# A linear recurrence with a routed expert layer on one core: early router rows searched per 256 columns, the last router step apart, weights and more zero fills inside a new hand-ordered list

## Chip, cores and metric

The kernel runs on one core of one Trainium2 chip. The metric is the device time of one execution in microseconds (us); less is better. The core has five engines with a queue each: TensorE (PE, with its weight loads shown as PEld), VectorE (DVE), ScalarE (ACT), GpSimd (POOL) and SyncE (SP), which here issues nearly all DMAs. Engines run their own queues in order and wait for each other by semaphores.

## What is computed

The input is a batch of 4 sequences of 5056 tokens with 256 channels, float32. First a gated linear recurrence runs over each sequence, and then its 20224 result rows go through a top-1 routed layer of 8 experts, in which each expert keeps only its 80 most certain tokens. All other output rows are zero.

```
sig_r, sig_i = sigmoid(r_gate), sigmoid(i_gate)
a_t = exp(8 * sig_r * log(sigmoid(a_param)))
x_gated = sqrt(max(1 - a_t*a_t, 1e-6)) * sig_i * x
h_t = a_t * h_(t-1) + x_gated_t             # along the sequence, per channel
logits = h @ w_gate                         # [20224, 8]
expert = argmax(logits);  gate = softmax(logits)[expert]
for each expert e: keep the 80 tokens of e with the largest gate
    out[token] = gate * (relu(h[token] @ w1[e]) @ w2[e])     # 256 -> 1024 -> 256
out[all other tokens] = 0
```

## The kernel before

**Data.** `Y` is one large SBUF tensor of 50 slots of 128 x 1024 float32. Slots 0 to 39 end up holding the recurrence's result, channel-major, in 40 units `u` of 512 tokens (the last has 256). Until then the slots hold loaded inputs and intermediate values; the tables `SLOTS` say which slot serves `r`, `i`, `x` and the decay `a` of each unit. Slots 40 to 49 are extra and later hold expert weights (`wbuf`, slots 40 to 47) and scratch (`scr`, slots 48 and 49).

**The main phase** is a list, `ORDER`, of tokens, each a task; every engine executes its part in the order of the list (`tc.manual_schedule`). SP's DMAs follow the same list. The tasks of unit u: `Lr`, `Li`, `Lx` load 512 KB each; `Tr` transposes r on PE into PSUM; `tr` is the tanh on ACT; `e` the decay (two Exp on ACT); `q` its square (POOL); `s` the root (ACT); `ti` a tanh of i (ACT); `u` or `v` the gated input, on POOL (L152, L153) or on DVE (L155); `Tu` transposes it on PE; `xg` multiplies by the norm (DVE L163); `y` is the scan (DVE L171), which carries its state from unit to unit. A number after the dot of `e`, `q`, `s`, `ti`, `u`, `v` says how many units one instruction covers. ACT pays a table load each time it changes between Exp/Tanh and Sqrt.

**The router.** `G` g forms logits of four units (2048 tokens) with eight matmuls in fp32 (two instructions each, L233). `R` s.k is stage k of router step s; a step covers two groups, so five steps cover ten groups (the last group has units 36 to 39):

```
stages = (r_copy, r_turn, r_max, r_exp, r_first, r_sum, r_recip, r_gate_, r_back, r_store)
```

They copy the logits to `lg` (ACT L237), transpose them (PE L241), find and subtract the maximum (DVE L252, L253), exponentiate (ACT L258), mark the first largest expert (DVE L262 to L264), add up and invert (POOL L269 to L272, DVE L275), multiply the mark with the gate (POOL L278), transpose back (PE L283) and store into `rows` (ACT L287). `rows` has 128 partitions (8 experts x 16, by token mod 16) and 1264 columns: 1024 "early" columns from groups 0 to 7, 240 late ones from groups 8 and 9, and between them 16 places (`K1`) for the largest early values. One PSUM tile (`ps_g`, one buffer) serves all steps, and one `lg`.

**The end of the list.** `T` (`early_top`) finds the 16 largest of the 1024 early columns of each partition: largest eight, their indices, replace, largest eight, indices (L292 to L294). `Z` writes 256 KB of zeros to the output (L218); 79 of them cover the output, 45 stand in the list, and the other 34 are issued after it, behind the first eight weight loads (L320, L323).

**After the list.** `top16` over the 16 early winners and 240 late columns gives 16 candidates per partition. Exact ranks among the 16 partitions of an expert follow (DVE L403, L410, ACT L404), a one-hot selection (DVE L420, PE L426), and a branch (L476) that jumps over a slow general path unless a partition could hold more chosen tokens than were searched. Then each of ACT, POOL and DVE reads its share of an expert's 80 column numbers into registers (L499, one register load of 28 or 24 values) and copies those columns one by one (L505, L506); PE multiplies (L520, L522) and POOL scatters the rows to the output (L533). Weights of experts 2 to 7 are loaded as buffers come free.

Of the kernel before, what the change touches and what calls it, by code (L numbers as in the profile page):

```python
# [15 lines left out]
P = 128  # L16
C = 512
# [7 lines left out]
STEPS = ((0, 1), (2, 3), (4, 5), (6, 7), (8, 9))  # L25
SLOTS = dict(r=(1, 2, 3, 4, 5, 10, 14, 16, 21, 22, 13, 24, 29, 31, 33, 27, 37, 38, 41, 21, 22, 35, 44, 45, 46, 30, 40, 48, 31, 33, 49, 43, 36, 46, 47, 44, 49, 43, 42, 47),
             i=(6, 8, 9, 19, 20, 9, 19, 27, 30, 20, 32, 34, 18, 19, 23, 20, 40, 34, 43, 32, 36, 24, 27, 33, 42, 32, 36, 47, 34, 44, 32, 41, 40, 48, 42, 45, 37, 46, 45, 48),
             x=(11, 13, 15, 8, 11, 23, 25, 15, 26, 28, 35, 36, 30, 25, 26, 18, 42, 28, 47, 29, 48, 25, 26, 43, 28, 38, 41, 29, 42, 45, 38, 34, 35, 41, 38, 40, 48, 41, 40, 44),
             a=(0, 7, 12, 17, 18, 6, 7, 8, 12, 9, 11, 17, 14, 15, 16, 19, 23, 17, 20, 31, 49, 34, 23, 37, 24, 25, 27, 35, 28, 37, 30, 31, 32, 33, 34, 35, 36, 38, 41, 39))
# [29 lines left out]
    xg36.1 y36.0 Z u38.1 R3.3 Tu37.0 Z tr38 R3.4 Tu37.1 Z tr39 Z e38.1 y36.1 Z Z xg37.0 e39.1 R3.5 Tu38.0 Z xg37.1 ti39.1 Z q38.1 y37.0 Z s38.1 R3.6
    Z Tu38.1 y37.1 R3.7 Z q39.1 Z R3.8 xg38.0 Z u39.1 xg38.1 Z s39.1 y38.0 Z Z R3.9 Tu39.0 y38.1 Tu39.1 Z G8 Z xg39.0 xg39.1 Z y39.0 Z y39.1 Z T Z  # L60
    G9 Z Z Z R4.0 Z R4.1 Z Z Z Z R4.2 Z R4.3 Z R4.4 R4.5 R4.6 R4.7 R4.8 R4.9
# [18 lines left out]
def moe_kernel(ctx, tc, x, r_gate, i_gate, a_param, w_gate, w1, w2, out, capacity=80):  # L80
# [14 lines left out]
    tiny = const.tile([P, 58], F32, name="tiny")  # L95
# [84 lines left out]
    mx = h1[:, 144:176]; sm = h1[:, 176:208]; total = h1[:, 208:240]  # L180
# [25 lines left out]
    eidx = tiny[:, 38:54].bitcast(U32); ecol = tiny[:, 22:38]  # L206
# [13 lines left out]
    st = {}  # L220
    LAST = -(-NU // 4) - 1
    exx = lg[:, C // 2:]
    def width(g): return min(512, (N - 2048 * g) // 4)
    def logits(g):

        s = plan.step_of[g]; k = g - plan.steps[s][0]; last = g == plan.steps[s][-1]
        if k == 0: st['pl'] = ps_g.tile([P, 512], F32, name="pl")
        us = range(4 * g, min(4 * g + 4, NU))
        for n in sorted({ntok(u) for u in us}, reverse=True):
            part = [u for u in us if ntok(u) == n]; c0 = (part[0] - 4 * g) * P; last_part = last and n == min(ntok(u) for u in us)  # L230
            for h in range(2):
                for j in range(4):
# [5 lines left out]
    def r_turn(s):  # L238
        st['pt'] = pt = st['pl'].rearrange("p (b k) -> p b k", b=4)
        w = width(plan.steps[s][0])  # L240
        for b in range(4): nc.tensor.transpose(pt[:w // 4, b], lg[:, b:w:4], ident)  # L241
# [351 lines left out]
```

## Time and profile before

| | us |
|---|---|
| median of 3 runs (lowest, highest) | 332.15 (331.56, 332.41) |
| the profiled execution, its own time | 329.29 |
| span of its trace (first to last instruction) | 327.5 |
| mean granted TensorE clock | 0.792 |

| engine | busy us | share of span |
|---|---|---|
| PE | 222.6 | 68% |
| DVE | 222.7 | 68% |
| ACT | 231.2 | 71% |
| POOL | 231.5 | 71% |

The DMAs moved 100.7 MB, 307 GB/s over the span; the queue of SP's DMAs was busy 86% of the time that 16 DMA engines have. The shares are averages over the main phase (to about 225 us), the router's end and the search (to about 251 us), a stretch with almost nothing (251 to 256 us), and the experts (to the end). So each stretch has to be read by itself. The TensorE clock is given as a share of full speed: 1.00 is 2.4 GHz and 0.50 is 1.2 GHz.

### The profile page before, as it was taken

The page shows a single profiled execution, that of the slowest core. Times are in us where ns is not written, and L with a number is a line of the kernel's source. Part 1 is how long each engine was busy: PE and PEld are TensorE (multiplying, and loading weights), DVE is VectorE, ACT ScalarE, POOL GpSimd, SP SyncE. Part 2 cuts the span into 40 slices and gives each one's busy share as a digit, 9 for nine tenths or more (in the row PEclk, how much of TensorE's full clock was granted, in tenths as well). Part 3 has the DMA queues.
Part 4 walks back from the last instruction along what each step waited for, and adds up shares of the span by engine and source line. Part 5 has one row for each costly group of instructions (what it writes and reads, how often), then busy time and mean ns, then how long its engine had stood idle before and what let it go on. Part 6 is the DMA issues. An engine that isn't in the chain of part 4 may idle for free. (4 is left out here: it accounts for less than half of the span.)

```text
span 327.5 us, 5668 instructions
## 1 busy us (share of the span) xinstructions
PE 222.6 (68%) x1400; PEld 169.1 (52%) x1400; DVE 222.7 (68%) x515; ACT 231.2 (71%) x454; POOL 231.5 (71%) x358
## 2 busy tenths in 40 slices
PE   3663838496669855798644776348253668999994
PEld 3562833255565343754523326222142558999994
DVE  1047978968579993998659796799684174466611
ACT  6999999989969999689659998891131063453500
POOL 2494999789699999799996989981253167453712
PEclk9957678578579995599975797957757675999999
DMA  7999999999987479896996879999999942999940
GB/s 251 409 404 345 385 412 410 409 370 393 366 327 234 162 260 372 274 309 220 313 366 215 277 208 355 392 374 296 370 375 375 335 165 67 301 353 336 343 149 20
DMA packets 52532, 100.70 MB, mean 307 GB/s; under 512 B 4368, under 2 KB 32912, under 8 KB 52496
## 3 DMA queue, kind: packets, MB, share of 16 engines
q1 hardware_dynamic: 52112, 99.64, 86.0%
q0 software_dynamic: 384, 0.66, 0.6%
q8 instruction: 13, 0.21, 0.3%
q14 instruction: 23, 0.19, 0.2%
HBM read 78.91 MB, written 21.36 MB: 306 GB/s over the span
## 5 line engine op out<-in xcount | busy, mean ns | idle before, releaser
L171 DVE TENSOR_TENSOR_SCAN Y<-Y,pu 128x512 f32<-128x512 f32 (+4 forms) x86 | 97.5, 1169 | 0.4
L160 PE MATMUL pu<-ident,Y 128*128 128x128 f32 x316 | 61.2, 334 | 44.9 <-DVE Y L171 33.6
L141 POOL TENSOR_TENSOR Y<-Y 128x1024 f32<-128x1024 f32 (+2 forms) x29 | 75.2, 2608 | 16.4 <-ACT Y L138 15.9
L160 PEld LDWEIGHTS pu<-ident,Y 128*128 128x128 f32 x316 | 44.4, 172 | 68.3 <-issue 46.3
L153 POOL TENSOR_TENSOR Y<-Y 128x1024 f32<-128x1024 f32 (+2 forms) x25 | 72.9, 2916 | 2.2 <-POOL Y L152 0.2
L124 PE MATMUL pr<-ident,Y 128*128 128x128 f32 x316 | 55.9, 341 | 26.9 <-DMA Y<-in_r_gate_dram 19.0
L124 PEld LDWEIGHTS pr<-ident,Y 128*128 128x128 f32 x316 | 49.1, 181 | 32.4 <-ACT Y L126 14.1
L163 DVE SCALAR_TENSOR_TENSOR pu<-Y,pu 128x512 f32<-128x512 f32 (+1 forms) x80 | 51.2, 676 | 16.5 <-ACT Y L144 11.7
L138 ACT ACTIVATE Y<-Y,tiny 128x512 f32<-128x512 f32 (+2 forms) x58 | 52.4, 961 | 3.0 <-POOL Y L271 2.4
L520 PE MATMUL ph<-Y 128*128 128x80 f32 x256 | 45.7, 273 | 4.4 <-DMA out_dram<-Y 3.0
L522 PE MATMUL po<-Y,rows 128*80 128x128 f32 x256 | 48.3, 282 | 0.0
L148 ACT ACTIVATE Y<-Y 128x1024 f32<-128x1024 f32 (+2 forms) x29 | 38.7, 1359 | 7.8 <-DMA Y<-in_i_gate_dram 7.6
L126 ACT ACTIVATE Y<-pr 128x1024 f32<-128x1024 f32 (+1 forms) x40 | 39.1, 1005 | 7.1 <-PE pr L124 7.1
L520 PEld LDWEIGHTS ph<-Y 128*128 128x128 f32 x256 | 40.6, 206 | 5.0 <-POOL Y L506 3.4
L505 ACT COPY Y<-Y 128x2 f32 x224 | 22.8, 191 | 26.2 <-issue 23.7
L506 POOL COPY Y<-Y 128x2 f32 x192 | 24.3, 200 | 24.0 <-issue 16.1
L152 POOL TENSOR_SCALAR Y<-Y 128x1024 f32<-128x1024 f32 (+2 forms) x25 | 33.8, 1352 | 9.7 <-ACT Y L148 7.3
L233 PE MATMUL pl<-Y 128*32 128x512 f32 (+2 forms) x176 | 37.3, 986 | 2.0 <-ACT rows L287 2.0
L144 ACT ACTIVATE Y<-Y 128x1024 f32<-128x1024 f32 (+2 forms) x32 | 38.0, 1248 | 0.4 <-POOL Y L141 0.3
L522 PEld LDWEIGHTS po<-Y,rows 128*80 128x80 f32 x256 | 29.8, 158 | 0.0
L506 DVE COPY Y<-Y 128x2 f32 x224 | 24.7, 178 | 7.2 <-issue 7.0
L155 DVE SCALAR_TENSOR_TENSOR Y<-Y 128x1024 f32<-128x1024 f32 x9 | 18.0, 2002 | 17.0 <-ACT Y L148 14.8
(131 smaller groups left out, 159.5 us busy)
## 6 DMA issues: line engine op xcount, KB each, us to landing
out_dram<-Y SPq DMA_DIRECT2D x79, 256.0 KB, 4.7
Y<-in_r_gate_dram SPq DMA_DIRECT2D x39, 512.0 KB, 6.3
Y<-in_i_gate_dram SPq DMA_DIRECT2D x39, 512.0 KB, 6.8
Y<-in_x_dram SPq DMA_DIRECT2D x39, 512.0 KB, 5.8
Y<-in_moe_w_dram SPq DMA_DIRECT2D x32, 512.0 KB, 5.0
Y<-in_r_gate_dram SPq DMA_DIRECT2D x1, 256.0 KB, 7.6
Y<-in_x_dram SPq DMA_DIRECT2D x1, 256.0 KB, 7.4
Y<-in_i_gate_dram SPq DMA_DIRECT2D x1, 256.0 KB, 5.2
```

The costliest lines, as they stand in the source:

```text
L124: nc.tensor.transpose(pr[:, h, b:nb * P:nb], rr[:, b, h * P:(h + 1) * P], ident)
L126: nc.scalar.activation(rslot(u), prs.pop(u)[:, :, :ntok(u)], AF.Tanh, scale=0.5)
L138: nc.scalar.activation(a[:, :, h], z[:, :, h], AF.Exp, scale=L[:, h:h + 1], bias=L[:, h:h + 1])
L141: nc.gpsimd.tensor_tensor(pair('r', u, m), a, a, op=ALU.mult)
L148: nc.scalar.activation(i, i, AF.Tanh, scale=0.5)
L153: nc.gpsimd.tensor_tensor(v, i, v, op=ALU.mult)
L160: nc.tensor.transpose(pu[:, b:nb * P:nb], tmb('x', u)[:, b, h * P:(h + 1) * P], ident)
L163: nc.vector.scalar_tensor_tensor(pu, rslot(u)[:, h], 0.5e-3, pu, op0=ALU.max, op1=ALU.mult)
L171: nc.vector.tensor_tensor_scan(y[:, s0:s1], a[:, s0:s1], q[:, s0:s1], init, op0=ALU.mult, op1=ALU.add)
L506: else: eng.tensor_copy(dst, src)
L520: nc.tensor.matmul(ph[:, c % (FC // 2)], w1v(e1)[:, h, c * P:c * P + P], XG[:, e1, h], start=(h == 0), stop=(h == 1))
L522: nc.tensor.matmul(po[:, h, :P], h2T[:, c], w2v(e2)[:, c, h * P:h * P + P], start=(c == 0), stop=(c == FC - 1))
```

## The change

1. `T` is gone. Behind router steps 0 to 3 a task `P` s finds the eight largest of that step's 256 columns and their indices. Near the end, `M0` (DVE) picks the 16 largest of the 4 x 8 = 32 values and marks which cell they come from, `M1` and `M2` (POOL) turn that into column numbers.
2. Eight per 256 columns may miss a ninth. The row's largest "eighth" is kept, and the flag for the general path is raised where a chosen candidate is not above it: on DVE a maximum, a comparison, a product and a sum stand where one comparison stood.
3. The last router step is split: step 4 has group 8 alone, step 5 group 9 alone, with its own PSUM tile and its own SBUF buffers (slot 49). Group 9's matmuls come in two parts, `Ga` for units 36 to 38 and `Gb` for unit 39 alone; `Ca` copies the first part. In step 5 the sum and the gate's product are on DVE.
4. The list is a new one throughout, with new slots. The 8 weight loads stand in it (`W0` to `W7`), and 63 zero fills, the first behind `xg14.0` (before: behind `y32.0`). Up to the last input load the list has 49 zero fills (before: 12), behind it 14 (before: 33), and 16 come after the list (before: 34). Tasks by kind, of those whose count changes:

| | e pairs, singles | s pairs, singles | ti pairs, singles | u pairs, singles (POOL) | v singles (DVE) |
|---|---|---|---|---|---|
| before | 11, 18 | 8, 24 | 11, 18 | 6, 19 | 9 |
| after | 10, 20 | 6, 28 | 10, 20 | 4, 21 | 11 |

In both lists ACT changes to the root's table 11 times.

```diff
-STEPS = ((0, 1), (2, 3), (4, 5), (6, 7), (8, 9))
+STEPS = ((0, 1), (2, 3), (4, 5), (6, 7), (8,), (9,))
...
-    Z Tu38.1 y37.1 R3.7 Z q39.1 Z R3.8 xg38.0 Z u39.1 xg38.1 Z s39.1 y38.0 Z Z R3.9 Tu39.0 y38.1 Tu39.1 Z G8 Z xg39.0 xg39.1 Z y39.0 Z y39.1 Z T Z
-    G9 Z Z Z R4.0 Z R4.1 Z Z Z Z R4.2 Z R4.3 Z R4.4 R4.5 R4.6 R4.7 R4.8 R4.9
...
+    u38.1 R3.8 y36.0 e38.1 Z Z y36.1 Tr39 R3.9 Z Tu37.1 tr39 xg37.0 G8 Z e39.1 q38.1 xg37.1 W0 s38.1 y37.0 q39.1 W1 y37.1 u39.1 P3 W2 Tu38.0 Tu38.1
+    s39.1 xg38.0 W3 R4.0 Tu39.0 xg38.1 R4.1 y38.0 Z W4 y38.1 Tu39.1 Z R4.2 Ga Z xg39.0 R4.3 xg39.1 y39.0 Z y39.1 W5 R4.4 R4.5 Gb Ca M0 W6 R5.0 R5.1
+    W7 R5.2 M1 Z R4.6 R5.3 R5.4 Z Z R5.5 R4.7 R5.6 M2 R4.8 Z R5.7 R5.8 Z R4.9 R5.9
 """
...
-    mx = h1[:, 144:176]; sm = h1[:, 176:208]; total = h1[:, 208:240]
+    mx = h1[:, 122:154]; sm = h1[:, 154:186]; total = h1[:, 186:218]
+    cell = h1[:, 218:250]; eighth = h1[:, 250:251]; cell0 = h1[:, 251:255]
...
+    def spread(g, units):
+        step = plan.step_of[g]; k = g - plan.steps[step][0]; last = g == plan.steps[step][-1]; final = units[-1] == min(4 * g + 3, NU - 1)
+        n = ntok(units[0]); c0 = (units[0] - 4 * g) * P
+        for h in range(2):
+            for j in range(4):
+                nc.tensor.matmul(st['pl', step][32 * j:32 * j + 32, c0:c0 + len(units) * n // 4], wg[:, h, E - E * k:E - E * k + 32],
+                                 Y[:, units[0]:units[-1] + 1, h, j:n:4], start=(k == 0 and h == 0 and c0 == 0), stop=(last and final and h == 1),
+                                 tile_position=(0, 32 * j))
...
+    def logits_first():
+        st['pl', LAST_STEP] = ps_r.tile([P, 2, C], F32, name="pr")[:, 0]
+        spread(LAST, list(range(4 * LAST, NU - 1)))
+    def logits_last(): spread(LAST, [NU - 1])
+    LAST_STEP = len(plan.steps) - 1; HEAD = (NU - 1 - 4 * LAST) * P
+    lgs = [lg] * LAST_STEP + [Y[:, NU + 9, 0]]
+    def copy_first():
+        nc.gpsimd.memset(ex9(P)[:, :, E:], 1e-9)
+        nc.scalar.copy(lgs[-1][:, :HEAD], st['pl', LAST_STEP][:, :HEAD])
...
+        if s == LAST_STEP:
+            nc.vector.tensor_reduce(out=total[:n, NR:2 * NR], in_=ex9(n), op=ALU.add, axis=AX.X)
+            return
...
+        (nc.vector if s == LAST_STEP else nc.gpsimd).tensor_tensor(keys(s), keys(s), by_expert(sm, s), op=ALU.mult)
...
-    def early_top():
-        top16(rows[:, :NE], rows[:, NE:NE + K1], eidx, rows[:, :NE])
-        nc.vector.tensor_copy(ecol, eidx)
...
+    def cell_top(s):
+
+        src, c = rows[:, 2 * P * s:2 * P * s + 2 * P], slice(8 * s, 8 * s + 8)
+        nc.vector.max(cell[:, c], src)
+        nc.vector.max_index(cidx[:, c].bitcast(U32), cell[:, c], src)
+    NC = 4 * 8
+    where = scr[:, 512:1024].rearrange("p (k q) -> p k q", q=NC)
+    pos, nth = scr[:, 256:272], scr[:, 288:288 + NC]
+    def merge(n):
+
+        if n == 0:
+            nc.vector.tensor_reduce(out=eighth, in_=cell[:, 7:NC:8], op=ALU.max, axis=AX.X)
+            nc.gpsimd.iota(nth, pattern=[[1, NC]], base=0, channel_multiplier=0, allow_small_or_imprecise_dtypes=True)
+            top16(cell, rows[:, NE:NE + K1], pos.bitcast(U32), cell)
+            nc.vector.tensor_tensor(where, pos.bitcast(U32).unsqueeze(2).broadcast_to([P, K1, NC]), nth.unsqueeze(1).broadcast_to([P, K1, NC]), op=ALU.is_equal)
+        pool = nc.gpsimd
+        if n == 1:
+            pool.tensor_copy(cidx, cidx.bitcast(U32))
+            by8 = cidx.rearrange("p (s k) -> p s k", k=8)
+            pool.tensor_tensor(by8, by8, cell0.unsqueeze(2).broadcast_to([P, 4, 8]), op=ALU.add)
+            pool.tensor_tensor(where, where, cidx.unsqueeze(1).broadcast_to([P, K1, NC]), op=ALU.mult)
+        if n == 2:
+            w = NC // 2
+            while w:
+                pool.tensor_tensor(ecol if w == 1 else where[:, :, :w], where[:, :, 0] if w == 1 else where[:, :, :w],
+                                   where[:, :, 1] if w == 1 else where[:, :, w:2 * w], op=ALU.add)
+                w //= 2
...
-    for e, g in ((0, 0), (0, 1), (1, 0), (1, 1)): load_w1(e, g)
-    for e, g in ((0, 0), (0, 1), (1, 0), (1, 1)): load_w2(e, g)
+    WLOADS = [(load, e, g) for load in (load_w1, load_w2) for e in range(2) for g in range(2)]
+    def weights(w):
+        load, e, g = WLOADS[w]
+        load(e, g)
...
+    full = small[:, 226:242]
+    nc.vector.tensor_tensor(eighth, eighth, cv[:, K - 1:K], op=ALU.max)
+    nc.vector.tensor_scalar(full[:, :K], cv[:, :K], eighth, None, op0=ALU.is_le)
...
-    nc.vector.tensor_scalar(fl, rk[:, K - 1:K], float(CAP), None, op0=ALU.is_lt)
+    nc.vector.scalar_tensor_tensor(lt[:, :K], rk[:, :K], float(CAP), full[:, :K], op0=ALU.is_lt, op1=ALU.mult)
+    nc.vector.tensor_reduce(out=fl, in_=lt[:, :K], op=ALU.add, axis=AX.X)
```

## Rows read from the trace of the kernel before

**Rows 1.** Four stretches of the main phase: from and to in us, length, busy us of PE, PEld, DVE, ACT and POOL in this order (each with its number of instructions), then the granted TensorE clock, the mean share of time in which the 16 DMA engines were busy, and GB/s.

```profile
0.00:100.00 100.00, 63.27 (x334) 50.36 (x334) 65.66 (x82) 92.08 (x85) 78.26 (x63) 0.74 0.97 373
100.00:140.00 40.00, 29.02 (x162) 19.18 (x161) 34.03 (x43) 36.31 (x37) 37.74 (x19) 0.79 0.77 259
140.00:208.00 68.00, 45.85 (x269) 27.27 (x268) 55.78 (x67) 57.88 (x61) 61.86 (x35) 0.84 0.84 287
208.00:225.40 17.40, 8.16 (x38) 4.11 (x40) 14.57 (x22) 14.05 (x19) 12.25 (x13) 0.62 1.06 374
```

**Rows 2.** Groups of instructions by line with their shapes kept apart, up to 226 us: count, busy us, mean ns of one, idle time before them and what ended it.

```profile
L138 ACT ACTIVATE Y<-Y,tiny 128x1024 f32<-128x1024 f32 x22 | 26.0, 1232 | 2.5 <-POOL Y L271 2.4
L138 ACT ACTIVATE Y<-Y,tiny 128x512 f32<-128x512 f32 x34 | 25.6, 807 | 0.5 <-DVE pu L163 0.3 <-POOL Y L153 0.2
...
L144 ACT ACTIVATE Y<-Y 128x1024 f32<-128x1024 f32 x23 | 23.1, 1047 | 0.1
...
L144 ACT ACTIVATE Y<-Y 128x2048 f32<-128x2048 f32 x8 | 15.1, 1903 | 0.0
...
L152 POOL TENSOR_SCALAR Y<-Y 128x1024 f32<-128x1024 f32 x18 | 20.8, 1155 | 7.3 <-ACT Y L148 7.3
...
L152 POOL TENSOR_SCALAR Y<-Y 128x2048 f32<-128x2048 f32 x6 | 12.4, 2063 | 2.4 <-DMA Y<-in_r_gate_dram 2.4
...
L153 POOL TENSOR_TENSOR Y<-Y 128x1024 f32<-128x1024 f32 x18 | 44.4, 2464 | 1.5
...
L153 POOL TENSOR_TENSOR Y<-Y 128x2048 f32<-128x2048 f32 x6 | 27.3, 4548 | 0.6 <-POOL Y L152 0.2
...
L155 DVE SCALAR_TENSOR_TENSOR Y<-Y 128x1024 f32<-128x1024 f32 x9 | 18.0, 2002 | 17.0 <-ACT Y L148 14.8 <-DMA Y<-in_x_dram 2.2
```

**Rows 3.** The timeline from the last scans to the search after the list, merged: start us, us, engine, line, operation and shapes, count, and in brackets the idle time before it and what ended it.

```profile
219.79 1.29 DVE L163 SCALAR_TENSOR_TENSOR pu<-Y,pu 128x512 f32<-128x512 f32 x2 [0.42 <-ACT Y L144]
...
224.00 1.38 DVE L171 TENSOR_TENSOR_SCAN Y<-Y,pu 128x256 f32<-128x256 f32 x2
...
225.29 1.20 DVE L292 MAX8 rows<-rows 128x8 f32<-128x1024 f32 x1
...
229.34 0.38 PEld L233 LDWEIGHTS pl<-Y 128*32 128x32 f32 x12 [0.53 <-issue]
230.06 0.59 ACT L237 COPY lg<-pl 128x512 f32<-128x512 f32 x1 [7.64 <-PE pl L233]
...
230.70 0.75 PE L241 MATMUL pl<-ident,lg 128*128 128x128 f32 x4 [0.71 <-ACT lg L237]
...
231.86 0.42 DVE L252 TENSOR_REDUCE Y<-pl 128x32 f32<-128x256 f32 x1
...
233.33 0.45 POOL L269 TENSOR_TENSOR lg<-lg 128x128 f32<-128x128 f32 x1 [11.41 <-ACT lg L258]
233.86 0.29 POOL L270 TENSOR_TENSOR lg<-lg 128x64 f32<-128x64 f32 x1
...
235.38 0.34 DVE L275 RECIPROCAL Y<-Y 128x32 f32<-128x32 f32 x1
235.81 0.62 POOL L278 TENSOR_TENSOR lg<-lg,Y 128x256 f32<-128x256 f32 x1 [1.03 <-DVE Y L275]
...
236.49 0.66 PE L283 MATMUL pl<-ident,lg 128*128 128x128 f32 x2 [5.04 <-POOL lg L278]
237.04 0.23 POOL L331 IOTA lg<- 128x128 int32 x1 [0.61 <-PE pl L283]
237.19 0.36 ACT L287 COPY rows<-pl 128x240 f32<-128x240 f32 x1 [3.94 <-PE pl L283]
...
237.71 0.42 DVE L292 MAX8 lg<-rows 128x8 f32<-128x256 f32 x1
...
238.25 0.42 DVE L293 FIND_INDEX8 lg<-lg,rows 128x8 uint32<-128x256 f32 x1
```

**Rows 4.** The same timeline further on: two instructions of the ranking, a small one and a wide one.

```profile
240.25 0.17 DVE L370 TENSOR_SCALAR lg<-lg 128x14 f32<-128x14 f32 x1
...
248.04 0.79 DVE L420 TENSOR_TENSOR Y<-lg 128x560 bf16<-128x560 f32 x1
```

**Rows 5.** The timeline of SP's queue: zero fills issued behind the last input load, and zero fills issued after the list.

```profile
207.41 17.59 SPq L218 DMA_DIRECT2D out_dram<-Y  x23
...
232.37 30.01 SPq L218 DMA_DIRECT2D out_dram<-Y  x34
```

**Rows 6.** One line's instructions by engine, for L499 (the register loads of the experts' columns) and L476 (the branch): operation, count, then duration in ns as min/median/max, and the start of the first and the last.

```profile
L499 DVEq TENSOR_LOAD <-lg x8: 1848/1852/4105, 256.8 to 304.1; - x8
L499 ACTq TENSOR_LOAD <-lg x8: 1713/1738/4342, 256.8 to 304.8; - x8
L499 POOLq TENSOR_LOAD <-lg x8: 1542/1568/3940, 256.8 to 304.4; - x8
...
L476 DVEq COMPARE_BRANCH  x1: 90/90/90, 251.5 to 251.5; - x1
L476 DVEq EVENT_SEMAPHORE  x1: 21/21/21, 255.9 to 255.9; - x1
```

**Rows 7.** Two stretches after the branch, among the experts, with the columns of rows 1.

```profile
270.00:277.00 7.00, 5.89 (x31) 5.92 (x31) 4.19 (x36) 1.52 (x14) 5.44 (x44) 0.50 0.26 76
281.00:284.00 3.00, 3.00 (x32) 3.00 (x32) 2.84 (x26) 1.02 (x10) 1.14 (x1) 1.00 1.04 309
```

More of the change, by code (lines that the diff above doesn't have):

```diff
@@ L221, in moe_kernel @@
     LAST = -(-NU // 4) - 1
-    exx = lg[:, C // 2:]
     def width(g): return min(512, (N - 2048 * g) // 4)
-    def logits(g):
[L226 to L232, printed above, removed]
-                    nc.tensor.matmul(st['pl'][32 * j:32 * j + 32, c0:c0 + len(part) * n // 4], wg[:, h, E - E * k:E - E * k + 32],
-                                     Y[:, part[0]:part[-1] + 1, h, j:n:4], start=(k == 0 and h == 0 and c0 == 0), stop=(last_part and h == 1),
-                                     tile_position=(0, 32 * j))
+    def spread(g, units):
[6 more added lines that the diff above has]
+                                 tile_position=(0, 32 * j))
@@ new lines, in logits @@
+    def logits(g):
+        step = plan.step_of[g]
+        if g == plan.steps[step][0]: st['pl', step] = ps_g.tile([P, 512], F32, name="pl")
+        spread(g, list(range(4 * g, 4 * g + 4)))
+    def logits_first():
[4 more added lines that the diff above has]
+    lgs = [lg] * LAST_STEP + [Y[:, NU + 9, 0]]
@@ L236, in r_copy, with turned @@
+    def copy_first():
+        nc.gpsimd.memset(ex9(P)[:, :, E:], 1e-9)
+        nc.scalar.copy(lgs[-1][:, :HEAD], st['pl', LAST_STEP][:, :HEAD])
     def r_copy(s):
-        nc.scalar.copy(lg[:, :width(plan.steps[s][0])], st['pl'][:, :width(plan.steps[s][0])])
+        w = slice(HEAD if s == LAST_STEP else 0, width(plan.steps[s][0]))
+        nc.scalar.copy(lgs[s][:, w], st['pl', s][:, w])
+    def turned(s): return st['pl', s].rearrange("p (b k) -> p b k", b=4)
     def r_turn(s):
-        st['pt'] = pt = st['pl'].rearrange("p (b k) -> p b k", b=4)
@@ L294, in top16 @@
             if r == 0: nc.vector.match_replace(tmp, val[:, sl], src, -1.0); src = tmp
[L295 to L312 removed]
+    F = w1.shape[2]; FC = F // P
     def slot(a, n): return Y[:, a:a + n].rearrange("p u h t -> p (u h t)")
@@ L323, in load_w2 @@
         nc.sync.dma_start(w2v(e)[:, c], w2[e].rearrange("(c p) d -> p c d", p=P)[:, c])
-    for e, g in ((0, 0), (0, 1), (1, 0), (1, 1)): load_w1(e, g)
-    for e, g in ((0, 0), (0, 1), (1, 0), (1, 1)): load_w2(e, g)
+    WLOADS = [(load, e, g) for load in (load_w1, load_w2) for e in range(2) for g in range(2)]
+    def weights(w):
+        load, e, g = WLOADS[w]
+        load(e, g)
+    tasks = {'Lr': lambda u: load('r', u, rf), 'Li': lambda u: load('i', u, jf), 'Lx': lambda u: load('x', u, xf),
+             'Tr': r_transposes, 'tr': r_tanh, 'e': decay, 'q': square, 's': root, 'ti': i_tanh, 'u': gated, 'v': gated,
+             'Tu': u_transposes, 'xg': normed, 'y': scan, 'G': logits, 'R': lambda s, k: stages[k](s), 'Ga': logits_first, 'Gb': logits_last, 'Ca': copy_first, 'P': cell_top, 'M': merge, 'W': weights, 'Z': lambda: zero_fill(1)}
+    with tc.manual_schedule(engines={E_.Activation, E_.PE, E_.DVE, E_.Pool}):
+        for n, (kind, *args) in enumerate(plan.order):
+            tasks[kind](*args)
+            if n == GATE_AT: nc.sync.dma_start(wg[:, :, E:2 * E], w_gate.rearrange("(h p) e -> p h e", p=P))
+    mstack.close()
+    CAP = capacity
+    assert 0 < CAP <= 80
+    tstack = ExitStack()
+    ps_t = tstack.enter_context(tc.tile_pool(name="ps_t", bufs=1, space=bass.MemoryType.PSUM))
     zero_fill(-(-N // ZERO_TOKENS))
```

119 lines of the change are left out of this document (56 added, 63 removed).

## The prediction

> **What bounds the kernel now.** I read the busy time by stretches first. Up to 208 us ACT is busy 92.08 of the first 100 us, 36.31 of the next 40 and 57.88 of the next 68; POOL is behind it at first and ahead of it from 100 us on, and the DMA engines are full at first and have room between 100 and 208 us [rows 1]. So the main phase hangs on ACT, POOL and the stream of loads together. From 208 us to the last scan DVE is the fullest engine, 14.57 of 17.40 us, and the reader is to see in the timeline that the one gap before the scans of unit 38 is 0.42 us [rows 1, 3].
>
> The timeline then shows a chain with one engine at a time. The last scan ends at 224.00 + 1.38 = 225.38. Group 9's matmuls end just before ACT's copy at 230.06, the router's ten stages follow one by one to 237.55, and the search over the late columns starts at 237.71 [rows 3]: 12.33 us from the last scan. `T`, which starts at 225.29, lies beside group 9's matmuls and hides behind them but for some tenths.
>
> The third view is the line of the branch and of the register loads. DVE branches at 251.5 and goes on at 255.9; the next thing is a register load on three engines at once, and its first execution takes 3.94 to 4.34 us where the median is 1.57 to 1.85 [rows 6]. SP's queue issues 34 zero fills from 232.37 to 262.38 [rows 5], across both. From 270 us on PE is the bound: in 281 to 284 us it is busy all the time at full clock [rows 7]. What comes after the register loads keeps its length and only shifts.
>
> **The change, part by part.** The sum is made against the profiled execution's 329.29 us; the median of the runs is 2.86 us above it, and I add the same sum to the median of 332.15.
>
> *A. From the last scan to the late search.* After the change the last scan is followed on DVE by R4.4 (three instructions on half the width), M0, R5.2, R4.6, R5.4 to R5.7. A DVE instruction of 256 elements takes 0.42, one of 14 takes 0.17 [rows 3, 4]; I price 128 elements in the middle, 0.29, bounds 0.17 and 0.42. R4.4: 0.9. M0: one small reduction, and the four searches and one replacement over 32 values with their value loads, 1.2, and a comparison of 512 elements priced as the 560 one, 0.8: 2.0. DVE is then at 2.9 us after the last scan. `Gb` hides under this: its 64-column matmuls come last in the group that ends at 230.06, the 12 weight loads at 229.34 among them, so they take under 0.7 us; a copy (under 0.59) and a turn of 0.75 follow [rows 3], 2.0 in all, and `Ga` has run while unit 39 was scanned. Without that cover `Gb` and its two steps would set the start of R5.2 instead, up to `Ga`'s length later. Then R5.2 0.6, R4.6 0.25, R5.4 0.9, R5.5 and R5.6 0.6, R5.7 0.3: 5.5. One transposition in place of two 0.4 and ACT's copy 0.36 [rows 3]: rows are ready at 6.4. But POOL now has M1, R4.7 and M2 after M0: 0.2 + 0.2 + twice the 0.62 of 256 elements, 0.45, then 0.62, 0.45, 0.29 and two of about 0.23, 3.9 us [rows 3]. It ends at 6.8, and the index patterns that POOL writes afterwards (0.23 at 237.04) and two small DVE steps stand ahead of the search in DVE's queue; the search would start at 7.7 if they stay in that order. I take 7.1, between 6.4 and 7.7. A = 7.1 - 12.3 = -5.2, bounds -4.6 and -5.9.
>
> *B. DVE ahead of the last scan.* P3 is a search and an index pass over 256 columns, 237.71 to 238.67 [rows 3], 0.96. It stands behind y37.1 and ahead of xg38.0, so the last scans queue behind it and behind its wait for ACT's store of step 3, which stands well ahead in the list. R4.2 adds two instructions, 0.6. Against it the gap of 0.42 can take part of P3, and the reciprocal of step 3 (0.34) now stands before y36.0. +0.8, bounds 0 and 1.5. P0 to P2 cost nothing: DVE is busy only 65.66, 34.03 and 55.78 us of 100, 40 and 68 [rows 1]. If that cover is gone, each costs 0.96.
>
> *C. The ranking* has three more small DVE instructions on its chain at 0.17 [rows 4]: +0.5 (0.4 to 0.6).
>
> *D. The first register load.* Behind the last input load the list of before issues 33 fills, and 34 follow: 67 x 0.262 MB and 4.2 MB of weights, 21.8 MB, 58 us at 374 GB/s from about 207.4 [rows 1, 5]. After the change there are 14 and 16 fills and the same weights, 12.1 MB, 32 us: they end near 240, or 245 if the load stream is late. The 8 weight loads wait in SP's queue for slots of unit 39, and only fills are queued behind them. DVE's branch comes at 251.5 - 5.2 + 0.8 + 0.5 + 1.3 (F) = 248.9, so the fills are over. The first load is the only one of eight on each engine that is slow, and the only one under the fills [rows 5, 6]: 4.1 to 1.85 on DVE, D = -2.3, bounds 0 (first executions are slow for another reason) and -2.6 (ACT's two numbers).
> The Trainium skill speaks against D: its page "SBUF — State Buffer", section "Who interferes with whom", says that DMA never contends with a compute engine. By that rule D is 0 and the sum below is -4.1; no run here shows yet which of the two holds for a register load.
>
> *E. The branch.* DVE stands 4.3 us between its branch and its next instruction, again under the fills [rows 5, 6]. Nothing in the trace shows how long it would be without them; bounds 0 and -4.3. I take about a third, -1.5.
> The Trainium skill, page "Runtime: NRT & Kernel Launch", section "Instruction fetch mechanics", says that a taken branch out of the fetched window has to fetch by DMA first; no run here shows that for this branch.
>
> *F. The main phase.* ACT gets one decay pair, two root pairs and one tanh pair less, and twice as many singles: 4 x 0.81 - 2 x 1.23 = 0.8, 4 x 1.05 - 2 x 1.90 = 0.4, and 0.2 for the tanh, priced like a root [rows 2]: +1.3, with the table changes the same. POOL loses two gated pairs and gets two singles: 7.2 - 13.2 = -6.0; DVE gets two gated singles of 2.0 more, +4.0 [rows 2], hidden in its idle time (if not, 4.0). The load stream has 37 more fills ahead of its end, 0.70 us each at 374 GB/s: 25.9 us. The room between 100 and 208 us is 0.23 x 40 + 0.16 x 68 = 20.1 us [rows 1], 5.8 less. So F lies between -6.0 (POOL was the bound) and +5.8 (the loads come late by all that doesn't fit). The loads run eight or more units ahead of the scans in the middle of the list, which can take 5.8 us; I take what ACT must do in any case, +1.3.
>
> Sum: -5.2 + 0.8 + 0.5 - 2.3 - 1.5 + 1.3 = -6.4. From 329.29 that is 322.9 profiled, and from the median 332.15 it is 325.8.
>
> **Rivals.**
> *1. The fills hold up the loads.* For it: SP's queue is one, and the fills stand between loads that wait for slots. Against it: the room of 20.1 us, and the lead of the loads. At 5.8 us it gives 325.8 + 4.5 = 330.3. The same mechanism ends on the other side: each fill ahead of a load that ACT waits for costs 0.70, and the gain is gone from a hold-up of 1.3 + 6.4 = 7.7 us, 11 fills of the 37. If half of them are not hidden, 13.0 us, the time is 337.5.
> *2. The stalls D and E are not due to the fills.* For it: a first execution, and a branch, may be slow by themselves. Against it: the same load is 2.3 us quicker seven times. Time 325.8 + 2.3 + 1.5 = 329.6. The skill's rule at D is this rival's, for D.
> *3. The flag fires and the general path runs.* It would search 1280 columns ten times over with three passes, each 1.20 x 1.25 [rows 3], 45 us, before anything else: over 370 us. Against it: with the reference's inputs no 256 columns of a row hold more than 7 chosen tokens, and it takes eight.
> *4. The clock.* PE multiplies at half clock from 270 to 277 us and at full clock later [rows 7]. The 5.89 us busy there would be about 3 at full clock, so a shorter pause ahead of it may give up to 3 us, and another turn of the clock may take as much. This is in the range, not in the sum.
>
> **How the numbers follow.** Forecast 0.53; rival 1 at 5.8 us 0.15, and from 7.7 us on 0.16; rival 2 0.14; rival 3 0.01; 0.01 for others. Faster or slower by 0.3% (1.0 us) is about what a measurement can tell. Faster are the forecast, most of rival 2 and most of the small rival 1: 0.75; within 0.3%, their edges: 0.08; slower, mostly the large rival 1: 0.17. The forecast's own range is 322 to 329 (F to -3, E to -2.5, or D and E halved with A at its low end). The range of 8 in 10 reaches down by half of F's POOL side and the rest of E, 325.8 - 4.3 - 2.5 = 319.0, and up over rivals 2 and 1 at 5.8 us: 332.0.
>
> **What would show it.** A: the late search's first pass starts 6.4 to 7.7 us after the last scan's end. B: that scan ends at 226 to 229 us. D: the maximum of L499's successor is below 2 us, and no fill is issued after 246 us. E: DVE's stand after its branch is 2 to 4 us. Wrong it would be if the last scan ended after 233 us, with ACT waiting for loads; if fills still ran at the branch; or if something ahead of the search, POOL's M2 above all, made A smaller than 4 us.

## Result and the profile after

The changed kernel takes 319.75 us (median of 4, 319.27 to 320.93) where the kernel before took 332.03 (331.56 to 332.41): ratio 0.9636, 95% interval 0.9605 to 0.9667. In a second group of runs, beside other kernels, it was 0.9652 (0.9596 to 0.9708). One of that group's six executions of the changed kernel took 374.67 us, about what rival 3 has for the general path; it left no trace, its cause is open, and it is not in the ratio. Of the two profiled executions the span falls from 327.5 to 317.6 us. The other 2 us of the medians' difference are in the runs and not in this pair: the profiled execution of before was 2.7 us quicker than its median.

The page's first lines after, then two stretches of the main phase with the columns of rows 1:

```profile
span 317.6 us, 5702 instructions
PE 215.5 (68%) x1404; PEld 161.7 (51%) x1404; DVE 229.9 (72%) x541; ACT 233.3 (73%) x463; POOL 228.1 (72%) x370
```

```profile
100.00:140.00 40.00, 27.67 (x171) 16.55 (x173) 36.24 (x46) 36.63 (x40) 35.10 (x20) 0.91 0.97 337
140.00:208.00 68.00, 43.99 (x251) 28.26 (x244) 58.61 (x74) 61.37 (x67) 60.66 (x38) 0.80 0.97 340
```

The DMA engines, busy 0.77 and 0.84 of these stretches before [rows 1], are at 0.97 in both. The next fence is the timeline from the last scan to the late search, and SP's zero fills behind the list:

```profile
223.59 1.38 DVE L172 TENSOR_TENSOR_SCAN Y<-Y,pu 128x256 f32<-128x256 f32 x2
...
226.14 17.73 SPq L221 DMA_DIRECT2D out_dram<-Y  x21
...
230.66 0.24 POOL L378 IOTA lg<- 128x128 int32 x1
...
230.93 0.33 DVE L379 TENSOR_SCALAR lg<-lg 128x128 int32<-128x128 int32 x1 [1.48 <-POOL lg L378]
231.19 0.28 DVE L285 TENSOR_TENSOR Y<-pr,Y 112x128 f32<-112x128 f32 x1
...
232.84 0.25 ACT L307 COPY rows<-pr 128x112 f32<-128x112 f32 x1 [2.51 <-PE pr L303]
233.12 0.43 DVE L312 MAX8 lg<-rows 128x8 f32<-128x256 f32 x1 [0.83 <-ACT rows L307]
```

From the last scan's end, 224.97, to the late search it is 8.15 us, before 12.33 [rows 3]. SP's last fill is issued by 243.9, before by 262.4 [rows 5]. The register loads (L550 after, L499 before) and the branch (L527, before L476), as in rows 6:

```profile
L550 DVEq TENSOR_LOAD <-lg x8: 1851/1856/1942, 250.4 to 294.2; - x8
L550 ACTq TENSOR_LOAD <-lg x8: 1730/1736/1914, 250.4 to 294.8; - x8
L550 POOLq TENSOR_LOAD <-lg x8: 1542/1566/1754, 250.4 to 294.5; - x8
...
L527 DVEq COMPARE_BRANCH  x1: 90/90/90, 246.6 to 246.6; - x1
L527 DVEq EVENT_SEMAPHORE  x1: 21/21/21, 249.5 to 249.5; - x1
```

No load is slow any more, and DVE stands 2.9 us behind its branch where it stood 4.4 [rows 6]. Put end to end, from the two timelines; the last column is the same difference between the second profiles of the two kernels, whose spans are 325.5 and 320.7 us:

| stretch | before | after | difference | second profiles |
|---|---|---|---|---|
| start to end of last scan | 225.38 | 224.97 | -0.4 | +2.9 |
| to the late search | 12.33 | 8.15 | -4.2 | -4.2 |
| to DVE's branch | 13.75 | 13.44 | -0.3 | -0.1 |
| DVE's stand | 4.44 | 2.93 | -1.5 | -1.2 |
| to the first expert products | 8.74 | 7.08 | -1.7 | -1.4 |
| to the first product with w2 | 6.93 | 6.10 | -0.8 | -0.8 |
| to PE's last | 51.39 | 50.37 | -1.0 | 0.0 |

Between the first expert products and the first product with w2, PE waits for the columns that DVE copies for the second expert, in both kernels (before, then after). So that stretch still belongs to DVE's register loads and copies, and not to PE:

```profile
271.11 0.68 PE L520 MATMUL ph<-Y 128*128 128x80 f32 x2 [1.40 <-DVE Y L506]
...
262.42 0.42 PE L571 MATMUL ph<-Y 128*128 128x80 f32 x2 [2.07 <-DVE Y L557]
```

The last stretch is PE among the experts, at half clock from 270 to 277 us before [rows 7], and for a shorter time after (columns of rows 1):

```profile
263.00:267.00 4.00, 4.00 (x26) 4.00 (x26) 3.07 (x27) 0.53 (x6) 2.68 (x23) 0.60 0.21 79
267.00:275.00 8.00, 8.00 (x82) 8.00 (x81) 4.24 (x33) 4.30 (x39) 3.73 (x23) 1.00 0.83 255
```

### The profile page after: what moved, and what is told of

It is laid out like the page before. It is cut to its first block, busy times and chain, and to the rows that moved or that the text cites. A ratio compares the mean times of both kernels' runs of the same rounds, so it can differ in the third digit from the quotient of the medians.

```text
span 317.6 us, 5702 instructions
## 1 busy us (share of the span) xinstructions
PE 215.5 (68%) x1404; PEld 161.7 (51%) x1404; DVE 229.9 (72%) x541; ACT 233.3 (73%) x463; POOL 228.1 (72%) x370
## 5 line engine op out<-in xcount | busy, mean ns | idle before, releaser
L142 POOL TENSOR_TENSOR Y<-Y 128x1024 f32<-128x1024 f32 (+2 forms) x30 | 74.2, 2485 | 27.3 <-ACT Y L139 27.2
L161 PE MATMUL pu<-ident,Y 128*128 128x128 f32 x316 | 57.2, 321 | 43.4 <-DVE Y L172 27.8
L161 PEld LDWEIGHTS pu<-ident,Y 128*128 128x128 f32 x316 | 42.4, 165 | 68.2 <-issue 31.9
L125 PE MATMUL pr<-ident,Y 128*128 128x128 f32 x316 | 53.3, 328 | 30.4 <-DMA Y<-in_r_gate_dram 23.5
L154 POOL TENSOR_TENSOR Y<-Y 128x1024 f32<-128x1024 f32 (+2 forms) x25 | 67.8, 2711 | 4.9 <-DMA Y<-in_x_dram 2.9
L125 PEld LDWEIGHTS pr<-ident,Y 128*128 128x128 f32 x316 | 45.9, 172 | 34.5 <-issue 18.9
L139 ACT ACTIVATE Y<-Y,tiny 128x512 f32<-128x512 f32 (+2 forms) x60 | 53.1, 944 | 2.6 <-DVE Y L156 2.2
L571 PE MATMUL ph<-Y 128*128 128x80 f32 x256 | 43.5, 262 | 2.3 <-DVE Y L557 2.1
L571 PEld LDWEIGHTS ph<-Y 128*128 128x128 f32 x256 | 38.6, 196 | 2.8 <-issue 2.8
L156 DVE SCALAR_TENSOR_TENSOR Y<-Y 128x1024 f32<-128x1024 f32 x11 | 25.3, 2304 | 17.5 <-ACT Y L149 13.1
L231 PE MATMUL pl<-Y 128*32 128x512 f32 x144 | 34.2, 1079 | 1.2 <-ACT rows L307 1.2
```

The lines of the kernel that those rows point to most:

```text
L125: nc.tensor.transpose(pr[:, h, b:nb * P:nb], rr[:, b, h * P:(h + 1) * P], ident)
L139: nc.scalar.activation(a[:, :, h], z[:, :, h], AF.Exp, scale=L[:, h:h + 1], bias=L[:, h:h + 1])
L142: nc.gpsimd.tensor_tensor(pair('r', u, m), a, a, op=ALU.mult)
L154: nc.gpsimd.tensor_tensor(v, i, v, op=ALU.mult)
L161: nc.tensor.transpose(pu[:, b:nb * P:nb], tmb('x', u)[:, b, h * P:(h + 1) * P], ident)
L571: nc.tensor.matmul(ph[:, c % (FC // 2)], w1v(e1)[:, h, c * P:c * P + P], XG[:, e1, h], start=(h == 0), stop=(h == 1))
```

## Experiments

**Fills put back behind the list.** The first 18 `Z` of the new list are taken out; the last call, which issues what is left, then issues them.

```diff
-    Tr21 R0.6 xg14.0 Z xg14.1 R0.7 ...
+    Tr21 R0.6 xg14.0 xg14.1 R0.7 ...          # and 17 more
```

> The changed kernel with the first 18 of its 63 listed zero fills taken out of the list, so that 34 fills are issued behind the list as in the kernel before (they then end near 256 us instead of 244). Everything else is as in the changed kernel. Theory (fills under the branch and the first register load make them slow): the first load of L550 rises from 1.87 to about 4.1 us on DVE, DVE's stand after its branch from 2.95 to about 4.4 us, the flag's own load from 0.56 to about 0.88; the first expert products start about 3.5 us later and the time rises by 3 to 5 us, to 323 to 325. Rival (they were slow for another reason, as a first execution): both stay at 1.87 and 2.95, and the time stays within 1 us of 319.8. Second question, the fills' price among the loads: with 18 fills fewer there the last scan, at 224.97 us in the changed kernel, should end up to 3 us earlier if they held up the loads, and within 0.5 us if they only filled idle time.

Measured: 323.6 us (321.7 to 326.5). The kernel before ran at 329.0 in this group, so the ratio says more: 0.985 (0.977 to 0.993), where the changed kernel has 0.964 and 0.965. SP's fills, then the register load and the branch under their line numbers here:

```profile
227.28 32.37 SPq L220 DMA_DIRECT2D out_dram<-Y  x39
...
L549 DVEq TENSOR_LOAD <-lg x8: 1848/1854/5261, 253.9 to 301.3; - x8
...
L526 DVEq COMPARE_BRANCH  x1: 90/90/90, 248.4 to 248.4; - x1
L526 DVEq EVENT_SEMAPHORE  x1: 21/21/21, 253.0 to 253.0; - x1
```

Both stalls are back, the load even at 5.26 us, and by the ratios the price is about 2%, an estimated 6 to 7 us, where 3 to 5 were expected. The last scan ends at 226.46, between the 224.97 and 227.83 of the changed kernel's two profiles: a price of the 18 fills in the new list doesn't show, but scans that end anywhere from 223.1 to 228.1 us with this list and its variants would hide one of some us.

**The kernel before without the fills behind its list, and with weight loads in their place.**

```diff
-    zero_fill(-(-N // ZERO_TOKENS))
+    pass                                                    # first kernel
+    for q in range(17): (load_w1, load_w2)[q // 4 % 2](q // 2 % 2, q % 2)   # second kernel
```

> The kernel before without the 34 zero fills that it issues behind its list; 43% of the output's zeros are left unwritten. Theory (fills cause the stalls): the first load of L499 falls from 4.1 to about 1.85 us, DVE's stand after the branch from 4.4 to about 2.9 us or less, and the time falls by 3.5 to 6 us, to 326 to 328.5. Rival (a first execution is slow by itself): both stay, and the time stays within 1 us of 332.

> The kernel before with the 34 zero fills behind the list replaced by 17 further loads of the first experts' weights, the same 8.9 MB in the other direction, from HBM into SBUF; 43% of the output's zeros are left unwritten. If it is the fills' reading of SBUF that slows the register load, the first load of L499 is at about 1.85 us as if there were no fills. If any full DMA queue slows it, it stays near 4.1 us. The stand after the branch, 4.4 us with fills, likewise: below 3 us or near 4.4. The time lies between that of the kernel before and that of the same kernel without the fills, unless the products wait for the last weights, which would show at the first instructions of L520.

Measured: 324.7 us without fills, ratio 0.988 (0.983 to 0.993), and 331.3 with weight loads, 1.014 (1.003 to 1.024). The first without fills, then with weight loads, and there the first products:

```profile
L499 DVEq TENSOR_LOAD <-lg x8: 1848/1853/1865, 255.4 to 300.3; - x8
...
L476 DVEq COMPARE_BRANCH  x1: 90/90/90, 251.3 to 251.3; - x1
L476 DVEq EVENT_SEMAPHORE  x1: 21/21/21, 254.5 to 254.5; - x1
```

```profile
L499 DVEq TENSOR_LOAD <-lg x8: 1848/1854/1984, 257.3 to 305.3; - x8
...
L476 DVEq COMPARE_BRANCH  x1: 90/90/90, 250.6 to 250.6; - x1
L476 DVEq EVENT_SEMAPHORE  x1: 21/21/21, 256.5 to 256.5; - x1
...
266.78 1.60 PE L520 MATMUL ph<-Y 128*128 128x80 f32 x7 [4.83 <-DMA Y<-in_moe_w_dram]
```

The register load is slow under the fills, 4.11 us, and not under as many bytes of loads from HBM into SBUF, 1.87. Whether it is their reading of SBUF, the one small tile of zeros that all of them read, or their writing to HBM isn't separated here. The branch goes otherwise: 3.25 us with neither, 4.44 under fills, 5.89 under weight loads (one profile). I had expected the two to behave alike; in these runs either traffic lengthens this stand, and the loads more. The time of the second kernel says nothing, since its products wait 4.83 us for the last weights.

The traces also hold what the stand waits for. In each of the thirteen, an 8 KB DMA packet of an instruction queue (the view's q14) starts within it, and DVE goes on 1.84 to 2.03 us after that start, however long the stand is. The queues' view of the kernel before, from 251.5 to 255.9 us, has it as one packet:

```profile
q14 instruction: 1, 0.01, 0.4%
```

What varies is the time from the branch to the packet: 1.06 to 1.64 us in the eight traces with little or no traffic there, 2.54 to 3.15 under fills, 3.86 under weight loads. The trace doesn't name the engine that a packet is for; that it is DVE's follows from this constant distance.

**The old early search in the new list.** P0 to P3, M1 and M2 leave the list, `T` stands for M0, and the flag is the old one.

```diff
-    ... Gb Ca M0 W6 R5.0 R5.1 W7 R5.2 M1 Z ... R5.6 M2 R4.8 ...
+    ... Gb Ca T W6 R5.0 R5.1 W7 R5.2 Z ... R5.6 R4.8 ...
```

> The changed kernel with the old early search: P0 to P3, M1 and M2 are gone, the old T over 1024 columns stands in M0's place, and the flag is the old one. The split of the last router step, the list and the fills stay. Theory (the search per 256 columns is worth its time only because the split step ends the cover of T): T takes 6.3 us on DVE where M0 takes 2.1, so the late search starts 3 to 4.3 us later than 233.12 and the time is 322.5 to 324. Rival (POOL's M1 and M2 and the waits behind them already cost what the cells save): within 1 us of 319.8.

Measured: 323.7 us (321.5 to 324.8), ratio 0.988 (0.981 to 0.996). DVE's timeline, last scan, start of T, late search:

```profile
224.43 1.38 DVE L171 TENSOR_TENSOR_SCAN Y<-Y,pu 128x256 f32<-128x256 f32 x2
...
226.56 1.22 DVE L311 MAX8 rows<-rows 128x8 f32<-128x1024 f32 x1
...
236.82 0.43 DVE L311 MAX8 lg<-rows 128x8 f32<-128x256 f32 x1 [0.82 <-ACT rows L306]
```

The stretch is 11.02 us, 2.9 longer. T holds DVE for 6.6 us ahead of R5.2; the wait for POOL's pattern, 1.48 us in the changed kernel, is gone in return. The time is in the range expected, but the ratio lies some 2.4% above the changed kernel's, about 8 us; beyond the 2.9 us of the stretch, nothing here shows where they are. The last scan ends at 225.80 without P3 ahead of it, within the new list's spread, so P3's price can't be read.

**One last router step.** The matmuls stay where the new list has them (`G8`, `Ga`, `Gb`), but groups 8 and 9 share a PSUM tile and their ten stages again.

```diff
-STEPS = (..., (6, 7), (8,), (9,))
+STEPS = (..., (6, 7), (8, 9))
-    ... Gb Ca M0 W6 R5.0 R5.1 ...
+    ... Gb M0 W6 R4.0 R4.1 W7 R4.2 M1 Z R4.3 R4.4 R4.5 Z Z R4.6 R4.7 Z M2 R4.8 Z R4.9
```

> The changed kernel with groups 8 and 9 in one last router step again (on the one PSUM tile, with lg, sum and gate on POOL), but with the matmuls where the changed list has them: group 8 early, units 36 to 38 beside unit 39's scan, unit 39 alone behind it. Search per 256 columns, fills and weights stay. Theory (the stretch from the last scan to the late search became shorter because the matmuls moved ahead and T is gone, and the split gives little): the stretch is 7.3 to 9.2 us, as the changed kernel's 8.15, and the time within 1.2 us of it. Rival (the split step with its shorter instructions is what shortened it): the stretch is 11 us or more and the time 3 us or more above.

Measured: 321.3 us (319.3 to 322.8), ratio 0.971 (0.964 to 0.978), beside 320.6 and 0.9652 for the changed kernel in the same group; the two intervals overlap.

```profile
221.74 1.38 DVE L171 TENSOR_TENSOR_SCAN Y<-Y,pu 128x256 f32<-128x256 f32 x2
...
230.96 0.36 ACT L305 COPY rows<-pl 128x240 f32<-128x240 f32 x1 [3.94 <-PE pl L301]
...
231.77 0.24 POOL L376 IOTA lg<- 128x128 int32 x1
...
232.04 0.25 DVE L377 TENSOR_SCALAR lg<-lg 128x128 int32<-128x128 int32 x1 [2.54 <-POOL lg L376]
...
232.47 0.42 DVE L310 MAX8 lg<-rows 128x8 f32<-128x256 f32 x1
```

The stretch is 9.35 us, a little above what was expected, and again it ends on POOL's pattern behind M2. So of 4.2 us the split gives 1.2 with the pattern where it is. ACT has stored the rows at 231.32 and the search starts only at 232.47; without the pattern in between, the split would be worth about 1.7 us (an estimate: 231.32 plus the 0.16 from store to search in [rows 3], less 223.12, is 8.4, and the kernel below, split and without this wait, has 6.72). The rest, by the rows, comes from matmuls that run ahead of the last scan instead of up to 230 us [rows 3]. Most of it needs T gone: with T the stretch is 11.02, only 1.3 below the 12.33 of before.

**The pattern moved.** POOL's pattern `se` gets columns of `lg` that are free early.

```diff
-    se = lg[:, :P]; iot = lg[:, P:P + 80]
+    se = lg[:, 384:512]; iot = lg[:, 0:80]
-    small = lg[:, 208:512]
+    small = lg[:, 80:384]
```

> The changed kernel with the 128 x 128 pattern of L378 to L380 in columns 384 to 511 of lg, which nothing uses after the turn of step 4, in place of columns 0 to 127, which step 4 uses to its end (the other tables in lg move with it). In the changed kernel DVE's L379 waits 1.48 us for POOL's L378 in the middle of step 5, with L285 of that step behind it. Theory (this wait is what made the stretch from the last scan to the late search 8.15 us where 7.1 was forecast): the stretch falls to 6.5 to 7.2 us and the time by 1 to 1.6 us. Rival (step 5 would then wait for step 4's end on POOL and PE in any case, since the late search needs both): the stretch stays above 7.7 us and the time within 0.5 us.

> The changed kernel once more, beside the others of this group. The first comparison gave a ratio of 0.964 to the kernel before; the profiled pair differs by less, 9.9 us of span. If the rest was chance of that chip, the ratio here is nearer 0.970; if the changed kernel is faster in all runs alike, it is 0.964 again.

> The changed kernel with the moved pattern once more, beside the next one. The stretch from the last scan to the late search is 6.7 us again and the ratio to the kernel before 0.960. Where the last scan ends tells how far the new list's main phase varies: it was at 224.97 and 227.83 us in the two profiles of the changed kernel, so anything from 223 to 228.

Measured: 318.5 us (315.7 to 320.4), ratio 0.9597 (0.9538 to 0.9655), beside 320.6 and 0.9652 for the changed kernel; in a later group 319.7, 0.9694 (0.9642 to 0.9745).

```profile
224.56 0.21 DVE L379 TENSOR_SCALAR lg<-lg 128x128 int32<-128x128 int32 x1
...
225.55 1.38 DVE L172 TENSOR_TENSOR_SCAN Y<-Y,pu 128x256 f32<-128x256 f32 x2
...
231.45 0.29 DVE L285 TENSOR_TENSOR Y<-pr,Y 112x128 f32<-112x128 f32 x1
...
233.65 0.43 DVE L312 MAX8 lg<-rows 128x8 f32<-128x256 f32 x1 [0.83 <-ACT rows L307]
```

L379 now runs before the last scan and waits for nothing. The stretch is 6.72 us, and 6.71 in the second profile: 1.4 us shorter, as expected, than the 8.15 that the changed kernel has in both of its profiles. Whether the kernel is faster the intervals leave open, since they overlap.

**Four matmuls in PE's pause among the experts.**

```diff
+        if k == -1:
+            pd = ps_f.tile([P, 512], F32, name="pd")
+            for _ in range(4): nc.tensor.matmul(pd[:, :256], ident, Y[:, 0, 0, :256], start=True, stop=True)
```

> The same kernel with four more matmuls on PE behind the first expert's first products (their result is not used), in the pause of 2.2 us in which PE waits for the second expert's columns. Theory (the pause sometimes drops the granted clock to half for the following products, which cost 1.7 to 3.4 us more then): no half-clock stretch from the first products to the end, and the stretch from the first product with w2 to PE's last is 48.7 us; the time is 0 to 1.5 us below the kernel without them. Rival (the clock falls for what PE did earlier, whatever fills the pause): half-clock stretches behind the pause as often as before, and the matmuls themselves delay the second products by up to 1.5 us when the clock is at half, so the time is equal or above.

Measured: 318.4 us, 0.9639 (0.9589 to 0.9689), beside 319.7 and 0.9694 without them; the intervals overlap. It tells nothing of the clock: from the first product with w2 to PE's last it is 48.74 us with them, and also 48.74 in both profiles without them; none fell to half clock there. The kernel without them from 263 to 267 us, where the changed kernel has a clock of 0.60 and 26 matmuls, has:

```profile
263.00:267.00 4.00, 3.54 (x35) 3.57 (x36) 2.19 (x21) 1.46 (x13) 2.69 (x22) 1.00 0.34 129
```

**18 fills early in the old list.** `Z` is put behind the scans of units 13 to 20.

```diff
+    ... y13.1 Z ... y14.1 Z ... y15.0 Z ... y15.1 Z Z Z Z Z Z ...      # 18 in all
```

> The kernel before with 18 more zero fills in its list, behind the scans of units 13 to 20 as in the changed kernel, and so 16 behind the list in place of 34; nothing else is changed. The fills then end near 250 us, about where DVE branches. Theory (the part of the gain that comes from the fills is had by moving them alone, and they cost nothing among the loads): the first load of L499 falls to about 1.86 us, DVE's stand after the branch to 3 to 4 us, the last scan still ends within 1.5 us of 225.4, and the time falls by 3 to 5 us. Rival (the fills hold up the old list's loads): the last scan ends 3 us or more later and the time falls by less than 1.5 us or rises.

Measured: 328.2 us, ratio 0.989 (0.985 to 0.994). Two stretches with the columns of rows 1, then load and branch:

```profile
100.00:140.00 40.00, 29.42 (x173) 19.46 (x172) 34.02 (x44) 35.69 (x35) 35.82 (x19) 0.80 0.96 340
140.00:208.00 68.00, 44.99 (x254) 26.38 (x252) 54.10 (x65) 58.34 (x63) 62.27 (x34) 0.80 0.78 272
```

```profile
L498 DVEq TENSOR_LOAD <-lg x8: 1849/1854/2792, 258.9 to 303.6; - x8
...
L475 DVEq COMPARE_BRANCH  x1: 90/90/90, 253.0 to 253.0; - x1
L475 DVEq EVENT_SEMAPHORE  x1: 21/21/21, 258.0 to 258.0; - x1
```

SP's queue here, from the last input load:

```profile
210.07 0.33 SPq L115 DMA_DIRECT2D Y<-in_i_gate_dram  x1
210.46 24.61 SPq L217 DMA_DIRECT2D out_dram<-Y  x32
...
242.20 16.71 SPq L217 DMA_DIRECT2D out_dram<-Y  x16
```

The time fell as expected by the ratio (the profiled pair shows only 0.5 us of it), and the last scan ended at 226.75, within the 1.5 us that were expected; the mechanism missed. The fills filled the room from 100 to 140 us, but the DMA share of the next stretch fell from 0.84 to 0.78, the last input load was issued at 210.1 instead of 207.0, and the fills still ran at the branch. The load fell half way only, the stand was 5.0. The queue shows why: 48 fills are left behind the last input load, where the kernel before has 57 [rows 5] and the changed kernel 30 (5, 1, 3 and the 21 behind its list). So 18 fills put early into the list took only 9 from the end, because the queue of the kernel before already issued 22 ahead of that load, though its list has 12 there. The changed kernel with its 18 fills late has 48 behind that load too, and both stalls. A late load is not what tells them apart: the changed kernel's last one is issued at 209.5.

**The kernel before, profiled again.**

> The kernel before once more, for a second profile of it. In the two kernels that left its list as it is, the last scan ended at 225.03 and 225.43 us, as in its first profile (225.38), so this one should end between 224.5 and 226.5, and the late search start 12.3 us later. The time is that of the kernel before, ratio 1.00 within the interval.

It was: 330.4 us, ratio 1.000 (0.995 to 1.004), last scan 224.90, late search 12.33 us later, first load 3.71, stand 4.39.

## Why the prediction was right, term by term

The direction and the range held (319.0 to 332.0), but the sum, -6.4, was little more than half of the -12.3 measured, or two thirds of the profiled pair's -9.9; the second profiles differ by 4.8. The time lies 0.75 us above the range's lower end. That end was reckoned from POOL's lighter work in the main phase and from nearly the whole stand; the stand gave no more than forecast, and nothing shows a gain from POOL, so it is partly luck that the time lies inside. Some 2 us of the -12.3 are in no trace.

- *A* was -5.2 and measured -4.2, in both pairs. The mechanism was seen, its size missed: 7.7 us was taken as the late end, with the pattern ahead of the search alone. In fact DVE's L379 sat in the middle of step 5 with L285 behind it. The moved pattern shows 6.72, within the forecast's 6.4 to 7.7. What A came from is corrected by the one-step kernel: less the shorter step than the matmuls moved ahead.
- *B and F*, +2.1 together, measured -0.4 in the first pair and +2.9 in the second. The old list ended its scans at 224.9 to 225.4 in four profiles, the new list and its variants at 223.1 to 228.1 in eight. The means are 0.7 us apart, and neither P3's price nor ACT's extra 1.3 us can be read from that. Why the new list varies so much is open. F's 37 further fills were counted in the list. SP is not among the engines that are held to the list's order, and in the traces 22 fills are issued ahead of the last input load before and 49 after: 27 more, 18.9 us at 0.70, which the room of 20.1 us holds. So the 5.8 us that didn't fit, and rival 1 at 5.8 us with them, had no ground.
- *C* was +0.5, measured -0.3 and -0.1. The small load of the flag, which I had not counted, fell from 0.88 to 0.56 us on DVE without the fills, and the three instructions cost about 0.1: with the old flag and no fills beside it the same stretch is 13.36 (the kernel with T), in the changed kernel 13.44.
- *D* was -2.3, and that is what it gave. The load itself fell by 2.2. To the first products alone the path fell by 1.7 only, but PE then waits for DVE; from DVE's resumption to the first product with w2 it was 15.67 us before and 13.18 after, in the second profiles 15.66 and 13.38, and 13.38 in the kernel before without fills. The reckoning of the fills' end was off: of the 33 fills behind the last input load, [rows 5] has 23, so 57 in all and not 67. A pause of 0.32 us of DVE ahead of its last two copied columns of the first expert stands in the changed kernel, with the moved pattern too, but neither in the kernel before without fills nor in those with T or with one last step; what makes DVE pause there is open. The Trainium skill's rule against D ("SBUF — State Buffer", section "Who interferes with whom"), if it is taken to cover a register load, is not borne out by the 4.11 and 1.87 us with and without fills.
- *E* was -1.5, a third of the stand taken without evidence, and measured -1.5 and -1.2: the size is luck. Some 3 us stay without any traffic, so the lower bound of -4.3 was out of reach. What traffic lengthens is the time to the instruction packet, 1.06 to 3.86 us from the branch. The Trainium skill, page "Runtime: NRT & Kernel Launch", section "Instruction fetch mechanics", says that a taken branch out of the fetched window has to fetch by DMA first. The packet in each of the thirteen stands agrees with that.
- *Rival 1* did not come at its size: in the old list 18 fills moved the last scan by 1.4 us, in the new one the spread hides what they cost. *Rival 2* is refuted by the kernel without fills. *Rival 3* shows in no trace: DVE is past its branch within 3.5 us in all seven of the changed kernel and its variants without late fills. *Rival 4*, the clock, was left out of the sum and gave -1.0 us in the first pair and nothing in the second, 50.12 and 50.15 us to PE's last; four profiles that stay at full clock there have 48.74.

## To carry to other kernels

Background writes out of SBUF aren't free while an engine reads registers from SBUF or jumps: end them before, or give them room elsewhere, and count in the queue's own trace how many are left behind the last load, since the order of a list need not be that of the queue. When a chain is shortened, look at what the scheduler puts into the engine's queue in the middle of it: one small wait in order cost as much as the split of the step gave. A hidden instruction (T) gets a price when its cover is taken away, so such edits have to be made together.

## What the runs showed of the hardware

A register load of 28 values took 1.85 us on DVE in the median and 1.87 under weight loads at full DMA rate; under zero fills it took 3.7 to 5.3 us, and up to 5.9 on ACT. A taken branch cost DVE 2.9 to 3.5 us with little or no DMA traffic beside it, 4.4 to 5.0 under zero fills, and 5.9 under loads from HBM. In all thirteen traces DVE went on 1.84 to 2.03 us after an instruction packet started, and the traffic delayed that packet.
